# Startup loads, block sizes, buffers, query order and DMA transposes changed together in a windowed-attention plus maxout feed-forward kernel

## The chip, the cores and the metric

The kernel runs on 1 core of one Trainium2 chip. The metric is the device time of one execution in microseconds (us); smaller is better. Engines are named as the profile names them: PE is TensorE's matmuls and PEld its weight loads, DVE is VectorE, ACT is ScalarE, POOL is GpSimd, SP is SyncE (here it only issues DMAs). L317 is line 317 of the kernel that the profile belongs to; the lines of the two kernels differ. The span is the time from the first to the last instruction. A row of slices cuts it into 40 equal parts; each digit is the busy share of a slice in tenths (9 is 90% or more). PEclk is the granted clock, the share of its full speed at which TensorE was allowed to run, in the same tenths; 1.00 is full speed. PSUM is the memory into which TensorE writes its results.

The kernel before takes 196.63 us, the median of the four runs beside the changed kernel (195.34 to 196.85). In longer sessions its executions fall into two groups: of twelve runs of one session six were fast (194.73 to 196.23) and six were called slow, being more than 1.5% above the fastest (197.99 to 200.0). The profiled execution that the prediction reads took 198.22 us and is of the slow group.

## The reference

Attention with a window of 128 keys and 4 sink keys, then a feed-forward layer in which three products compete by maximum:

```python
def _attn_ref(q, k, v, n_sink, window):         # q, k, v: (4, 8, 768, 64) float32
    scores = scale * np.matmul(q, k.transpose(0, 1, 3, 2))
    keep = is_sink | in_window                   # first 4 keys, or 0 <= q - k < 128
    scores = np.where(keep, scores, -1000000000.0)
    a = softmax(scores)                          # written out in the reference
    return np.matmul(a, v)

def _moe_ref(x, w1, w2, w3, w_out):              # x: (3072, 512), w1..w3: (512, 768), w_out: (768, 512)
    h = np.maximum(np.maximum(x @ w1, x @ w2), x @ w3)
    return h @ w_out
```

## The kernel before

The work is cut into 24 tiles of 128 tokens. For two tiles (a chunk of 256 tokens) and one of two head groups of four heads, a unit does: load q and k, transpose them on VectorE, scores on TensorE (`st`), exp on ScalarE, mask on VectorE, PV on TensorE (`o`), normalisation on VectorE (`x`), transpose of x on TensorE (`xt`), copy to `xT` on ScalarE. Some tiles make a block; for a block the feed-forward runs 18 groups of four `h` matmuls and then six `y` matmuls for each tile. Every operation is a task with a wanted time; a small list scheduler in the kernel decides the order in each engine's queue, and each engine works its queue strictly in that order.

```python
    NBUF = 4                                    # chunk buffers of each of q and k
    vbufs = [const.tile([128, H, 6, D + 1], BF16, name=f"v_sb{n}") for n in range(2)]
...
    load("q0.0", 0.26, -2000, qk_first("q", q, 0), eng="SP", cost=2.7)    # first chunk, head group 0
    load("k0.0", 0.26, -2000, qk_first("k", k, 0), eng="ACT", cost=2.7)
    qk_loads(0, 1)                                                        # head group 1, by GpSimd
    t_mask = task("POOL", 2.1, make_masks, want=nxt(), name="mask")
    v_loads(0)
    w_loads(0)
    ...
    for g in range(NQ):
        qk_loads(1, g)
...
    def transposes(ch, g, wants):               # VectorE, on pairs of bf16 taken as one float32
        for nm, want in zip("qk", wants):
            def f(nm=nm):
                src = raw(nm, ch, g).bitcast(F32).rearrange("p (j c) -> p j c", j=8)
                dst = tile_T(nm, ch, g).rearrange("p s e -> p (s e)").bitcast(F32).rearrange(
                    "p (m j) -> p j m", j=8)
                nc.vector.transpose(dst, src)
...
        def xt_copy():
            n = 128 * len(tts)
            src = st["xt"][:, :, 128 * tts[0]:128 * tts[0] + n]
            nc.scalar.copy(xT_tile()[:, 2 * g:2 * g + 2, off:off + n], src)

        def xt_dma(tt):                         # there, but used by no block: FIRST_BY_DMA = 99
            def f():
                o = off + 128 * (tt - tts[0])
                nc.sync.dma_start_transpose(out=xT_tile()[:, :, o:o + 128],
                                            in_=xs_tiles[ch, tt].rearrange("p h d -> p (h d)"))
...
        def store(m):
            def f():
                r = tok0 + 128 * m
                nc.sync.dma_start(out=out[r:r + 128, :], in_=box["ysb", m])
...
BLOCKS = [[0, 1], [2, 3], [4, 5, 6, 7], [8, 9, 10, 11], [12, 13, 14, 15], [16, 17, 18, 19], [20, 21, 22, 23]]
```

GpSimd issues all loads but the first two, with at most eight of them outstanding.

The softmax here doesn't subtract the row's maximum and nothing guards it: scores larger than these inputs give would overflow.

## Time and profile before

| kernel before, profiled execution | |
|---|---|
| span (first to last instruction) | 196.5 us |
| TensorE matmuls busy | 171.2 us, 87% |
| VectorE busy | 129.1 us, 66% |
| ScalarE busy | 95.5 us, 49% |
| GpSimd busy | 55.7 us, 28% |
| first matmul | 9.82 us |
| first y matmul | 38.57 us |

No single share says what bounds the kernel. TensorE is the busiest engine, but its 87% is an average of a first half with holes and a second half that is full. The lines that show it, with their reading, stand in the prediction: the slices, TensorE's waits, the timeline of the hole at 67 to 70 us, and the groups of instructions.

### The profile page before, as it was taken

The numbers are of one execution on the slowest core, as the hardware profiler recorded it, in microseconds if no ns is written. First come the engines' busy times: TensorE is split into PE (matmuls) and PEld (weight loads), VectorE is DVE, ScalarE is ACT, GpSimd is POOL, SyncE is SP. The second block draws the span as 40 slices with busy tenths as digits, with TensorE's granted clock in tenths as the row PEclk, the third lists the DMA queues.
The fourth block names the chain that finished last, engine by engine and source line by source line (L and its number), as shares of the span: only waits on it lengthen the run. The fifth ranks groups of instructions, "written<-read, shape, count | busy, mean of one in ns | idle before, by whom it ended". The sixth has DMA issues, their size and how long they took to land.

```text
span 196.5 us, 4237 instructions
## 1 busy us (share of the span) xinstructions
PE 171.2 (87%) x1659; PEld 95.6 (49%) x1680; DVE 129.1 (66%) x289; ACT 95.5 (49%) x147; POOL 55.7 (28%) x83
## 2 busy tenths in 40 slices
PE   0067978399999779999999999999999999999992
PEld 0044766148764335554445644555544556444440
DVE  4457768539999188998499962896915588135520
ACT  3263555436673606775175374736861573432222
POOL 7996759343692260059120000000000000000000
PEclk9999999969999969999999999999999999999999
DMA  5999999999999969099992023000041000230014
GB/s 113 127 162 164 196 182 173 172 136 215 127 135 136 139 69 175 24 71 142 243 153 43 3 81 132 3 0 3 0 168 49 2 3 0 107 112 0 0 53 160
DMA packets 58964, 19.52 MB, mean 99 GB/s; under 512 B 44352, under 2 KB 55616, under 8 KB 58944
## 3 DMA queue, kind: packets, MB, share of 16 engines
q0 software_dynamic: 54592, 12.40, 71.6%
q1 hardware_dynamic: 4160, 6.59, 9.4%
q10 hardware_dynamic: 192, 0.26, 0.4%
q8 instruction: 13, 0.21, 0.4%
q14 instruction: 7, 0.06, 0.1%
HBM read 25.17 MB, written 6.29 MB: 160 GB/s over the span
## 4 chain that ended last, share of the span: by engine, by line
PE 47%; DMA 27%; issue 11%; POOL 9%; SPq 3%; DVE 1%; ACT 0%; POOLq 0%; ACTq 0%
PE h L562 29%; DMA q_raw<-in_q_dram 16%; PE y L581 11%; DMA v_sb<-in_v_dram 6%; DMA w_sb<-in_moe_w_dram 5%; SPq L335 3%; PE o L442 3%; PE st L412 2%; POOL w_sb L199 2%; POOL v_sb L290 2%; PE xt L471 2%; POOL q_raw L188 1%; POOL k_raw L188 1%; PE o L433 1%; POOL v_sb L194 1%
## 5 line engine op out<-in xcount | busy, mean ns | idle before, releaser
L562 PE MATMUL h<-xT,w_sb 128*128 128x512 bf16 (+1 forms) x489 | 106.4, 355 | 3.0 <-DMA w_sb<-in_moe_w_dram 1.1
L573 DVE TENSOR_TENSOR h_sb<-h,h_sb 128x512 bf16<-128x512 f32 (+1 forms) x84 | 51.3, 610 | 35.5 <-PE h L562 32.1
L562 PEld LDWEIGHTS <-w_sb 128*128 128x128 bf16 x504 | 46.5, 100 | 39.2 <-issue 2.9
L417 ACT ACTIVATE e_sb<-st 128x1024 bf16<-128x1024 f32 (+1 forms) x48 | 44.0, 953 | 16.7 <-PE st L412 15.8
L571 ACT CAST h_sb<-h 128x512 bf16<-128x512 f32 (+1 forms) x42 | 22.1, 526 | 41.5 <-PE h L562 41.5
L581 PE MATMUL y<-wo_sb,h_sb 128*128 128x512 bf16 x138 | 34.3, 394 | 3.5 <-DMA wo_sb<-in_moe_w_out_dram 3.1
L424 DVE TENSOR_TENSOR e_sb<-e_sb,mask 128x1024 bf16<-128x1024 bf16 (+1 forms) x48 | 29.7, 638 | 2.4 <-ACT e_sb L417 2.4
L412 PE MATMUL st<-qT,kT 32*128 32x128 bf16 (+1 forms) x512 | 15.4, 248 | 9.9 <-DVE kT L302 9.8
L581 PEld LDWEIGHTS <-h_sb 128*128 128x128 bf16 x144 | 14.1, 101 | 19.6 <-issue 5.3
L588 ACT COPY y_sb<-y 128x512 f32<-128x512 f32 x24 | 14.1, 587 | 19.5 <-PE y L581 17.1
L302 DVE STREAM_TRANSPOSE qT<-q_raw 128x256 f32<-128x256 f32 x24 | 15.0, 633 | 11.8 <-DMA q_raw<-in_q_dram 11.8
L461 DVE TENSOR_TENSOR x<-o,rc 128x256 bf16<-128x256 f32 x48 | 20.4, 425 | 1.7
L442 PEld LDWEIGHTS <-e_sb 128*128 128x128 bf16 x352 | 16.9, 99 | 8.9 <-DVE e_sb L424 2.5
L483 ACT COPY xT<-xt 128x512 bf16<-128x512 bf16 x24 | 14.1, 588 | 13.9 <-PE xt L471 13.7
L442 PE MATMUL o<-v_sb,e_sb 128*128 128x65 bf16 x352 | 18.9, 197 | 1.6 <-DVE e_sb L424 1.4
L188 POOL DMA_DIRECT2D k_raw<-in_k_dram x23 | 15.6, 678 | 14.0 <-DVE x L461 4.5
L188 POOL DMA_DIRECT2D q_raw<-in_q_dram x23 | 15.9, 691 | 12.9 <-DVE h_sb L573 4.3
L412 PEld LDWEIGHTS <-kT 32*128 32x128 bf16 x512 | 10.2, 96 | 15.0 <-DVE kT L302 9.8
L302 DVE STREAM_TRANSPOSE kT<-k_raw 128x256 f32<-128x256 f32 x24 | 14.7, 627 | 1.1 <-DMA k_raw<-in_k_dram 1.1
L471 PE MATMUL xt<-ident,x 128*128 128x128 bf16 x96 | 12.3, 229 | 1.7 <-DVE x L461 1.7
L290 POOL DMA_DIRECT2D v_sb<-in_v_dram x6 | 8.7, 1445 | 13.9 <-PE st L412 11.9
L471 PEld LDWEIGHTS <-x 128*128 128x128 bf16 x96 | 7.7, 100 | 9.4 <-DVE x L461 3.6
(34 smaller groups left out, 48.3 us busy)
## 6 DMA issues: line engine op xcount, KB each, us to landing
out_dram<-y_sb SPq DMA_DIRECT2D x24, 256.0 KB
q_raw<-in_q_dram POOLq DMA_DIRECT2D x23, 128.0 KB, 9.6
k_raw<-in_k_dram POOLq DMA_DIRECT2D x23, 128.0 KB, 8.8
w_sb<-in_moe_w_dram POOLq DMA_DIRECT2D x9, 256.0 KB, 8.1
v_sb<-in_v_dram POOLq DMA_DIRECT2D x6, 384.0 KB, 11.5
vbd<-v_sb SPq DMA_DIRECT2D x64, 0.5 KB
v_sb<-in_v_dram POOLq DMA_DIRECT2D x6, 128.0 KB, 7.6
wo_sb<-in_moe_w_out_dram POOLq DMA_DIRECT2D x1, 768.0 KB, 10.0
```

Source lines behind the costliest of these rows:

```text
L188: nc.gpsimd.dma_start(out=raw(nm, ch, g), in_=s)
L302: nc.vector.transpose(dst, src)
L412: nc.tensor.matmul(ps[:, i, col:col + n], lhsT=kk[r, k0:k0 + 128, e], rhs=qT[r, q0:q0 + n, e], start=(e == 0), stop=(e == 1))
L417: nc.scalar.activation(st["e"][:, :, cols(tt)], st["ps"][:, :, cols(tt)], AF.Exp, scale=scale)
L424: nc.vector.tensor_tensor(out=ee, in0=ee, in1=m.unsqueeze(1).to_broadcast(list(ee.shape)), op=ALU.mult)
L442: nc.tensor.matmul(o[:, i, :], lhsT=st["e"][:, i, col:col + 128], rhs=vbufs[b % 2][:, 4 * g + i, kb, :], start=(c == 0 and n == 0), stop=( ...
L461: nc.vector.tensor_tensor(out=x, in0=o[:, :, :D], in1=rc.unsqueeze(2).to_broadcast([128, 4, D]), op=ALU.mult)
L471: nc.tensor.transpose(st["xt"][:, n, 128 * tt:128 * tt + 128], x[:, 128 * n:128 * n + 128], ident)
L562: nc.tensor.matmul(ps[:, :ntok], lhsT=w_sb[:, wi, d, fb * 128:fb * 128 + 128], rhs=xTs[blk][:, d, :ntok], start=(d == 0), stop=(d == DSUB ...
L571: nc.scalar.copy(hs, ps[:, :ntok])
L573: nc.vector.tensor_tensor(out=hs, in0=ps[:, :ntok], in1=hs, op=ALU.max)
L581: nc.tensor.matmul(ps, lhsT=box["h"][:, fb, 128 * m:128 * m + 128], rhs=wo_sb[:, fb, :], start=(fb == 0), stop=(fb == FSUB - 1))
```

## The change

The intent is to start sooner, to keep TensorE supplied until all loads are in, and to take work off TensorE where it is the bound. Six things change at once:

- q and k of the first chunk come for both head groups in four pieces each over three queues (SP, ACT, GpSimd), and the masks are built mostly by VectorE;
- the loads are reordered: chunk 1 before the first input weights;
- eight chunk buffers instead of four, and v of all four batches in tiles of its own;
- blocks of 2, 2, 2, 4, 4, 4, 4, 2 tiles instead of 2, 2, 4, 4, 4, 4, 4;
- x of the last three blocks (10 tiles) is transposed by DMA;
- the queries are in a permuted order within a tile, so that VectorE's transpose writes runs of 16 words; ScalarE's copy of x undoes the order, and in the DMA-transposed blocks the store of y undoes it.

```diff
+    load("q0.0", 0.26, -2000, qk_first("q", q, 0, nc.sync), eng="SP", cost=1.8)
+    load("k0.0", 0.26, -2000, qk_first("k", k, 0, nc.scalar), eng="ACT", cost=1.8)
+    load("q0.1", 0.26, -1999, qk_first("q", q, 1, nc.sync), eng="SP", cost=1.8)
...
-    NBUF = 4
+    NBUF = 8
-    vbufs = [... for n in range(2)]
+    vbufs = [... for n in range(B)]
...
-    qk_loads(0, 1)
-    t_mask = task("POOL", 2.1, make_masks, want=nxt(), name="mask")
+    load("k0.1", 0.26, nxt(), qk_first("k", k, 1, nc.gpsimd), cost=2.4)
     v_loads(0)
-    w_loads(0)
     for g in range(NQ):
         qk_loads(1, g)
     v_loads(1)
+    w_loads(0)
...
+                if nm == "q":
+                    dst = dst.rearrange("p (s j m) -> p j s m", s=2, j=8)
+                    src = src.rearrange("p (j s m) -> p j s m", j=8, s=2)
...
-            nc.scalar.copy(xT_tile()[:, 2 * g:2 * g + 2, off:off + n], src)
+            src = st["xt"][...].rearrange("p n (s j m) -> p n s m j", j=8, m=16)
+            dst = xT_tile()[...].rearrange("p n (s m j) -> p n s m j", j=8, m=16)
+            for t in range(len(tts)):
+                nc.scalar.copy(dst[:, :, t], src[:, :, t])
...
-                nc.sync.dma_start(out=out[r:r + 128, :], in_=box["ysb", m])
+                to = out[r:r + 128, :]
+                if blk >= FIRST_BY_DMA:
+                    to = to.rearrange("(m j) d -> j m d", j=8)
+                nc.sync.dma_start(out=to, in_=box["ysb", m])
...
-BLOCKS = [[0, 1], [2, 3], [4, 5, 6, 7], [8, 9, 10, 11], ..., [20, 21, 22, 23]]
-LEAD = 6.0
-FIRST_BY_DMA = 99
+BLOCKS = [[0, 1], [2, 3], [4, 5], [6, 7, 8, 9], [10, 11, 12, 13], [14, 15, 16, 17], [18, 19, 20, 21], [22, 23]]
+LEAD = 5.0
+FIRST_BY_DMA = 5
```

Cut from it: the mask code, the cost figures of the scheduler's model (which also move the order a little), and options that are switched off in both kernels (`N_BY_PE`, `TWO`).

## The prediction

> **What bounds the kernel now.** I read the page's slices first, then TensorE's waits, then 5 us stretches around each wait, then the timeline inside the worst one, then the groups of instructions. The slices (40 of 4.9 us, busy in tenths):
>
> ```profile
> PE   0067978399999779999999999999999999999992
> ...
> PEclk9999999969999969999999999999999999999999
> DMA  5999999999999969099992023000041000230014
> ```
>
> Two kernels stand one after the other here. From slice 21 (about 100 us) TensorE is full at full clock and the DMA engines are nearly idle. Before that TensorE has holes, the DMA row is at 9, and the two places where the granted clock falls come just behind holes. For the second part the busy table says the same in one line (columns: span, then busy us of PE, PEld, DVE, ACT, POOL, then clock):
>
> ```profile
> 100.00:193.00 93.00, 92.23 (x785) 47.61 (x796) 57.84 (x119) 45.32 (x71) 0.67 (x1) 1.00 0.17 48
> ```
>
> Only less TensorE work can shorten those 93 us. Most of what is lost lies before. TensorE's own waits up to 100 us:
>
> ```profile
> PE st L412 <- DVE kT L302: 9.8, 1, 9.8
> PE y L581 <- DMA wo_sb<-in_moe_w_out_dram: 3.1, 1, 3.1
> PE o L433 <- DVE h_sb L573: 1.9, 1, 1.9
> ```
>
> The first is the start: TensorE can begin at 9.82 us, when the last of four query/key transposes is done. The second is the arrival of the output weights at 38.57 us: block 0 is finished and its output product stands in front of everything else. The third is named "DVE h_sb", but the timeline shows what held VectorE:
>
> ```profile
> 66.38 1.02 PE L562 MATMUL h<-xT,w_sb 128*128 128x512 bf16 x4
> ...
> 68.10 0.64 DVE L302 STREAM_TRANSPOSE qT<-q_raw 128x256 f32<-128x256 f32 x1 [4.16 <-DMA q_raw<-in_q_dram]
> 68.59 0.67 DVE L573 TENSOR_TENSOR h_sb<-h,h_sb 128x512 bf16<-128x512 f32 x1
> ...
> 69.31 0.27 PE L433 MATMUL o<-vbd,e_sink 128*128 128x260 bf16 x1 [1.90 <-DVE h_sb L573]
> ```
>
> VectorE stood 4.16 us at the head of its queue on a transpose whose query chunk had not landed, the maxima behind it could not empty PSUM, and TensorE stopped. The chunk was issued at 58.66 and took 9.4 us to land, which is the median for queries (9.6); what was late is the issue: with four buffers per stream GpSimd waited there, the timeline says, for a transpose of VectorE. Both holes have an echo:
>
> ```profile
> 35.00:40.00 5.00, 1.80 (x28) 0.91 (x18) 1.98 (x6) 1.94 (x2) 1.43 (x3) 0.91 2.16 167
> 40.00:45.00 5.00, 5.00 (x45) 2.74 (x44) 2.62 (x7) 2.54 (x6) 2.00 (x3) 0.75 3.42 137
> ...
> 65.00:70.00 5.00, 2.88 (x37) 1.59 (x31) 1.90 (x5) 2.52 (x3) 1.58 (x3) 0.98 1.06 117
> 70.00:75.00 5.00, 4.58 (x32) 2.01 (x35) 4.37 (x11) 0.79 (x2) 1.74 (x3) 0.68 0.72 78
> ```
>
> The stretch after each hole runs at clock 0.75 and 0.68.
>
> **What the Trainium skill says.** (1) "TensorE: Matmul & The Clock Gate", What's actually happening: the default state is throttled, activity releases it, and an idle window brings it back. The trace agrees in kind: full clock elsewhere, 0.75 and 0.68 after the holes at 35 to 38.6 and 67 to 70 us. (2) "DMA: Bandwidth & Descriptors", Issuing engines are not separate DMA queues: starting DMAs from several engines only saves issue time. The trace before cannot show it for the first loads, but its DMA row is at 9 from slice 2 to slice 15, so three queues should bring the first tiles sooner and the last of the startup bytes no sooner. (3) "VectorE: DVE Perf Modes", The three transpose paths: a 128x128 bf16 transpose takes 390 ns on TensorE, 1309 ns on the DMA crossbar. The trace has 229 ns per transpose matmul and no DMA transpose; a longer latency off the engines is what the change buys.
>
> **The unit costs.** From spacings in the timeline at full clock: h matmul of 512 columns 0.216 us (72 from 172.03 to 187.57), of 256 columns 0.110 (8 from 50.76 to 51.64), y 0.216; scores of one unit (4 heads, one chunk) 0.57, or 0.46 in the first chunk of a batch; PV of a 128-token tile 0.37, in first chunks about 0.19; one transpose pair 0.11; sink scores 0.35. Total: h 432 x 0.216 = 93.3; y 144 x 0.216 = 31.1; scores 16 x 0.57 + 8 x 0.46 = 12.8; PV 32 x 0.37 + 16 x 0.19 = 14.9; transposes 48 x 0.11 = 5.3; sinks 5 x 0.35 = 1.8. Sum 159.2 us. Of it 14.8 lie before 38.57 us (72 h of 256 columns 7.9, six score units 3.2, eight PV tiles 2.2, seven pairs 0.8, two sinks 0.7). The other 144.4 take from 38.57 to 193.0, 154.4 us: 10.0 lost. Of these 2.5 are the hole at 67 to 70, and the clock costs (1 - 0.92) x 21.4 = 1.7 from 38.6 to 60 and (1 - 0.91) x 20 = 1.8 from 60 to 80; 4.0 are small waits.
>
> **The change part by part.**
> - Start. First chunks of both head groups come over SP, ACT and GpSimd, and VectorE transposes head group 0 first (in the kernel before, group 1's pair went first and TensorE used group 0). The casts end at 7.43 and 7.94; two transposes at 0.5 us spacing let TensorE start at about 8.6, some 1.2 us sooner. The masks, 6 GpSimd instructions of 0.3 us, become 2 there and 4 on VectorE, which idles 3.9 us then: free.
> - Order of loads. The bytes up to the output weights are the same 11 MB (six q/k groups, v of batch 0, all weights), and the DMA engines are full, so the weights should still land near 38.5. But block 2 is now 256 tokens and TensorE's order puts 108 h matmuls, not 72, before the first y: 36 x 0.11 = 4.0 us, plus one transpose pair 0.1. TensorE was ready at 35.4 and will start 1.2 sooner, so it is ready at about 38.3: the 3.1 us wait is filled, and 18.9 us of work are done at 38.6.
> - Buffers. With eight chunk buffers and all four v tiles no load waits for a transpose or a PV. The hole at 67 to 70 (2.5 us) goes, and with both holes most of their clock loss: I keep 1.0 of 3.5 us.
> - DMA transposes. Blocks 5 to 7 are 10 of 24 tiles: 20 pairs x 0.11 = 2.2 us less on TensorE, in the stretch where it is the bound, so it counts in full. ACT loses 10 copies of 0.588 us; the other 14 become 28 smaller ones (about 0.37 each, the duration of a 128x256 cast), 10.4 for 8.2 us: no matter at 49% busy.
> - Permuted queries. They let x come out in an order that ACT's copy or the store undoes; VectorE's query transpose then writes runs of 16 words. No row shows what that saves; I take nothing.
> - Blocks of 256: two more, 144 matmuls x (0.110 - 0.108) = 0.3 us more.
>
> Sum: remaining after 38.6 = 159.2 - 2.2 + 0.3 - 18.9 = 138.4. Lost: small waits 4.0, clock 1.0. TensorE ends at 38.6 + 143.4 = 182.0. The tail after it (last y copy and store, 3.5 us) stays: span 185.5. The timed median stands 0.3 over the span before: 185.8.
>
> **The rivals.**
> (a) VectorE takes over between 30 and 66 us. These are the rows:
>
> ```profile
> L573 DVE TENSOR_TENSOR h_sb<-h,h_sb 128x256 bf16<-128x256 f32 x24 | 10.0, 417 | 3.9 <-PE h L562 3.0 <-DVE h_sb L573 0.5
> L424 DVE TENSOR_TENSOR e_sb<-e_sb,mask 128x1024 bf16<-128x1024 bf16 x40 | 26.7, 682 | 0.7 <-ACT e_sb L417 0.7
> L302 DVE STREAM_TRANSPOSE qT<-q_raw 128x256 f32<-128x256 f32 x24 | 15.0, 633 | 11.8 <-DMA q_raw<-in_q_dram 11.8
> ```
>
> By the changed order VectorE has, from block 0's last maximum to block 2's, 24 maxima (10.0 us), 16 transposes (spaced 0.49 back to back: 7.8), 11 + 2 masks (8.3), 13 normalisations of 0.60 (7.8), 2 small ones: 34 us. TensorE has 31 for the same. For it: VectorE would end near 64, just where TensorE's own sum ends, so any wait for a chunk costs. Against it: it had 9 us of idle there before. I add 0.7 to the centre; fully, it makes 189.
> (b) The DMA transposes are late. Between the last PV of each of blocks 5, 6 and 7 and its first h stand 24 y matmuls, 5.2 us, in which normalisation (1 us), issue and transfer of the last tile must pass. If one takes over 4 us, each of three blocks loses 1 to 3 us, plus clock: 189 to 193. The skill's 1309 ns per 128x128, four to a tile but over 16 engines, speaks for it being tight but enough.
> (c) The wait only moves: the startup is bound by bytes, w_in for block 0 now comes after chunk 1, and v's 256-byte pieces are slow. If the output weights slip by 3 us, 189. If the DMA runs better than before (fewer issue waits), 183.
>
> **Range and chances.** Centre 186.5. Rivals (a) to (c) each add about 3 and rarely all together; below, nothing beats 138.4 + 3.5 after a landing near 38, about 180. Range 182 to 191.5. Faster by over 2% means under 192.9: 0.91; within 2% 0.08; slower 0.01, which would need transposes that stall every block.
>
> **What would show it.** Right: first matmul near 8.6; the first y right at the landing of the output weights, without 3 us idle; no wait of VectorE for q_raw over 2 us after 40; clock at 0.9 or more in every slice after the start; 56 transpose matmuls instead of 96; the stretch after 100 us full. Wrong: waits of h on the DMA transposes (b), VectorE above 95% between 40 and 66 with TensorE waiting for h_sb (a), or a first y much after 39 (c).

## The result, and the profile after

The changed kernel takes 190.13 us (median of four runs, 189.62 to 191.62, all fast). The ratio to the kernel before is 0.9695, with a 95% interval from 0.9623 to 0.9767. Here and below a ratio is the mean time of one kernel's fast runs over that of the other's of the same rounds, so it is not quite the ratio of the medians. The profiled execution took 190.57 us and has a span of 188.9 us.

The slices of the changed kernel, 40 of 4.7 us, answer to the three rows that the prediction shows of before:

```profile
PE   0267898899899999999999999999999999999970
...
PEclk9999999999999999999999999999999999999996
DMA  5989999999999999999997011250040440014403
```

The two dips of the granted clock are gone; only the last slice, in which TensorE has finished, is lower. The holes of TensorE are gone too: from the fifth slice on no digit is under 8 until the end. The DMA row is full until about 100 us, as before. The last digits differ: TensorE's row ends with "70", where before ended with "92", so the changed kernel has a longer stretch at the end in which TensorE does nothing.

Busy time in three stretches (columns: span, then busy us and instructions of PE, PEld, DVE, ACT and POOL, then clock, DMA share, GB/s):

```profile
30.00:40.00 10.00, 8.64 (x130) 6.59 (x128) 7.34 (x20) 5.30 (x12) 5.25 (x7) 1.00 1.55 176
40.00:69.20 29.20, 27.88 (x395) 20.98 (x398) 25.22 (x69) 18.68 (x37) 18.21 (x24) 1.00 2.09 153
69.20:183.00 113.80, 112.84 (x976) 60.50 (x989) 77.53 (x171) 53.22 (x87) 17.48 (x23) 1.00 0.58 84
```

The clock is full in all three. From 69.2 us, the first y matmul of block 2, TensorE is busy 112.84 of 113.8 us. Between 40 and 69.2 us VectorE is busy 25.22 of 29.20 us (86%), below the 95% that the prediction named as the sign of rival (a).

The waits (engine, line, what it waited for; us in all, times, longest):

```profile
PE st L435 <- DVE kT L317: 7.3, 1, 7.3
DVE qT L317 <- DMA q_raw<-in_q_dram: 3.4, 4, 1.2
...
PE h L588 <- DVE h_sb L602: 1.0, 2, 0.7
```

The start is at 7.3 instead of 9.8 us. VectorE's waits for query chunks fall from 11.8 us with a longest of 4.2 to 3.4 us with a longest of 1.2. The 3.1 us wait of y for the output weights is no longer among the waits of over half a microsecond. No wait of h for a DMA transpose is in the list.

The permuted order shows in the duration of VectorE's query transposes (before: 633 ns, shown in the prediction), and the two small copies of x in ScalarE's group:

```profile
L317 DVE STREAM_TRANSPOSE qT<-q_raw 128x256 f32<-128x256 f32 x24 | 10.3, 432 | 4.5 <-DMA q_raw<-in_q_dram 3.4
...
L510 ACT COPY xT<-xt 128x256 bf16<-128x256 bf16 x28 | 9.1, 380 | 7.0 <-PE xt L495 7.0
L495 PE MATMUL xt<-ident,x 128*128 128x128 bf16 x56 | 7.7, 231 | 1.6 <-DVE x L485 1.5
```

The end needs a closer look. The timeline of the changed kernel's last 9 us (start, duration, engine, line, operation), then that of the kernel before:

```profile
180.18 2.75 PE L616 MATMUL y<-wo_sb,h_sb 128*128 128x512 bf16 x11
...
182.33 1.89 SPq L633 DMA_DIRECT2D out_dram<-y_sb  x2
183.02 0.59 ACT L623 COPY y_sb<-y 128x512 f32<-128x512 f32 x1 [0.71 <-PE y L616]
```

```profile
189.72 4.22 SPq L595 DMA_DIRECT2D out_dram<-y_sb  x4
...
193.00 0.59 ACT L588 COPY y_sb<-y 128x512 f32<-128x512 f32 x1 [0.71 <-PE y L581]
```

After: the last copy ends at 183.61 and the span at 188.9, 5.3 us later. Before: the last copy ends at 193.59 and the span at 196.5, 2.9 us later. The DMA engines' busy share over the last stretch shows most of it; first the changed kernel from 170 to 189 us, then the kernel before from 180 to 197 us, each in 40 slices:

```profile
DMA  0670443555455454542000000000253455452000
```

```profile
DMA  0000000000000000000000001940950950950000
```

Each store of before is a short burst in which nearly all engines work: 9 tenths, up to 386 GB/s. The permuted stores of after never pass 5 tenths and 207 GB/s in these slices, so they last twice as long and run into each other. (The digits 6 and 7 at the start of the first row belong to a DMA transpose.) The Trainium skill, "DMA: Bandwidth & Descriptors", section "Why a DMA increments its semaphore by 16 and not by 1", says that a transfer is spread over the largest number of engines, at most 16, that divides the slowest dimension of both its sides. The permuted output `j m d` has 8 as its slowest dimension, so 8 of 16 engines. The trace agrees: half the busy share, half the rate. A small part, 0.26 us, is the issue: the last two stores of the changed kernel occupy SyncE from 182.33 us for 1.89 us, those of e3 below, with plain stores and the same two copies in front, for 1.63 us.

### The profile page after: what moved, and what is told of

Read it like the earlier page. It is cut to its first block, busy times and chain, and to the rows that moved or that the text cites. A ratio compares the mean times of both kernels' runs of the same rounds, so it can differ in the third digit from the quotient of the medians.

```text
span 188.9 us, 4359 instructions
## 1 busy us (share of the span) xinstructions
PE 167.7 (89%) x1693; PEld 100.4 (53%) x1712; DVE 128.3 (68%) x307; ACT 91.3 (48%) x158; POOL 63.2 (33%) x93
## 4 chain that ended last, share of the span: by engine, by line
PE 62%; DMA 21%; POOL 7%; DVE 4%; issue 2%; ACT 0%; DVEq 0%; ACTq 0%; POOLq 0%
PE h L588 38%; DMA q_raw<-in_q_dram 15%; PE y L616 14%; DMA w_sb<-in_moe_w_dram 6%; PE st L435 4%; PE o L466 4%; POOL w_sb L204 2%; POOL v_sb L199 2%; DVE h_sb L602 2%; PE o L457 1%; POOL k_raw L183 1%; PE xt L495 1%; DVE kT L317 1%; DVE x L485 1%; DVE e_sb L448 1%
## 5 line engine op out<-in xcount | busy, mean ns | idle before, releaser
L588 PE MATMUL h<-xT,w_sb 128*128 128x256 bf16 (+1 forms) x565 | 105.1, 331 | 2.6 <-DVE h_sb L602 1.0
L602 DVE TENSOR_TENSOR h_sb<-h,h_sb 128x256 bf16<-128x256 f32 (+1 forms) x96 | 52.7, 554 | 32.9 <-PE h L588 20.6
L588 PEld LDWEIGHTS <-w_sb 128*128 128x128 bf16 x576 | 54.2, 100 | 37.0 <-issue 2.8
L597 ACT CAST h_sb<-h 128x256 bf16<-128x256 f32 (+1 forms) x48 | 23.2, 484 | 45.3 <-PE h L588 45.2
L199 POOL DMA_DIRECT2D v_sb<-in_v_dram x24 | 21.9, 913 | 7.3 <-DMA q_raw<-in_q_dram 3.7
L317 DVE STREAM_TRANSPOSE qT<-q_raw 128x256 f32<-128x256 f32 x24 | 10.3, 432 | 4.5 <-DMA q_raw<-in_q_dram 3.4
L485 DVE TENSOR_TENSOR x<-o,rc 128x256 bf16<-128x256 f32 x28 | 11.9, 424 | 1.0
L510 ACT COPY xT<-xt 128x256 bf16<-128x256 bf16 x28 | 9.1, 380 | 7.0 <-PE xt L495 7.0
L476 DVE RECIPROCAL rc<-o 128x4 f32<-128x4 f32 x48 | 8.3, 174 | 3.5 <-PE o L466 3.5
L495 PE MATMUL xt<-ident,x 128*128 128x128 bf16 x56 | 7.7, 231 | 1.6 <-DVE x L485 1.5
```

Of the source, the lines that this page charges most:

```text
L199: nc.gpsimd.dma_start(out=vbufs[b][:, :, n, :D], in_=s[:, n])
L588: nc.tensor.matmul(ps[:, :ntok], lhsT=w_sb[:, wi, d, fb * 128:fb * 128 + 128], rhs=xTs[blk][:, d, :ntok], start=(d == 0), stop=(d == DSUB ...
L597: nc.scalar.copy(hs, ps[:, :ntok])
L602: nc.vector.tensor_tensor(out=hs, in0=ps[:, :ntok], in1=hs, op=ALU.max)
```

## The experiments

Twelve kernels ran, all with right results. "Control" is the unchanged changed kernel, run again in the first session: 190.82 us. The other sessions have no control, but the kernel before ran in each, and the mean of its fast runs was 195.3 to 195.6 us in all four (196.4 beside the first result), so times of different sessions are compared directly. Most edits are relative to the changed kernel. The first table gives times, the second milestones of the profiled executions.

| run | edit | median (range) us | ratio [95%] |
|---|---|---|---|
| e1 | none (control) | 190.82 (190.13 to 191.67) | 0.9773 [0.9738, 0.9809] |
| e3 | natural query order, DMA transposes kept | 188.26 (187.74 to 189.56) | 0.9652 [0.9611, 0.9694] |
| e2 | last block: order undone in h's operand | 215.52 (214.62 to 217.22) | 1.1042 [1.099, 1.1094] |
| e4 | no DMA transposes | 192.09 (191.58 to 192.91) | 0.9841 [0.981, 0.9873] |
| e7 | head group 1's first chunk by plain GpSimd loads | 194.52 (193.99 to 196.3) | 0.9972 [0.987, 1.0075] |
| e8 | load order of before | 191.68 (190.67 to 192.22) | 0.9792 [0.9717, 0.9866] |
| e10 | block sizes of before | 200.84 (200.49 to 201.78) | 1.0285 [1.0213, 1.0357] |
| e5 | four chunk buffers | 190.66 (190.31 to 191.22) | 0.9748 [0.9678, 0.9818] |
| e6 | four chunk buffers and two v tiles | 191.01 (189.35 to 191.64) | 0.975 [0.9665, 0.9836] |
| e11 | kernel before with the new buffers only | 197.93 (197.46 to 198.27) | 1.0127 [1.0059, 1.0196] |
| e9 | twelve maxima moved partly to ScalarE | 191.71 (191.04 to 195.82) | 0.9786 [0.9685, 0.9887] |
| e12 | e3 plus block 4 by DMA, and a split last tile | 197.93 (196.26 to 198.88) | 1.0121 [1.0053, 1.0189] |

| us | first y | first y of block 2 | last y group starts | last two apart |
|---|---|---|---|---|
| changed kernel | 40.05 | 69.20 | 180.18 | 110.98 |
| e1 | 39.24 | 69.91 | 180.89 | 110.98 |
| e3 | 40.45 | 69.27 | 180.25 | 110.98 |
| e5 | 39.92 | 69.70 | 180.68 | 110.98 |
| e6 | 40.92 | 69.91 | 180.90 | 110.99 |
| e7 | 40.57 | 72.83 | 183.35 | 110.52 |
| e8 | 37.06 | 69.23 | 181.25 | 112.02 |
| e9 | 40.15 | 69.97 | 181.60 | 111.63 |
| e4 | 39.48 | 69.54 | 183.85 | 114.31 |

The second table is worth keeping in mind for what follows. With the new block sizes and the DMA transposes, the stretch from block 2's first y to the last y group is 110.5 to 112.0 us in all rows whose x still goes by DMA. So an edit that acts early counts mainly if it moves that point, which stands near 69 to 70 us in all rows but one; in e8 and e9 about 1 us was lost after it.

### e1: the control

> Control: the changed kernel once more, as the yardstick of this job. Both theories: 190.1 us, within 1. In its profile 5.4 us from the end of the last y copy to the end of the span, against 2.9 in the kernel before.

The span is 189.6 us; the last copy ends at 184.31, 5.3 us before the end, as in the first profile. The long tail is no accident of one execution. The gain over the kernel before is 2.3% beside this control, with six fast runs of each, and 3% beside the first result, with four of each; the two intervals just overlap, so the gain is better put at 2 to 3%.

### e3: natural query order

```diff
-                base=0, pattern=[[1, 8], [8, 16]], channel_multiplier=-1)     # mask in permuted order
+                base=0, pattern=[[16, 8], [1, 16]], channel_multiplier=-1)    # in natural order
-                if nm == "q":        # the permuting pattern of the query transpose
+                if False:
-            for t in range(len(tts)):
-                nc.scalar.copy(dst[:, :, t], src[:, :, t])
+            nc.scalar.copy(xT_tile()[:, 2 * g:2 * g + 2, off:off + n], st["xt"][...])
-                if blk >= FIRST_BY_DMA:
-                    to = to.rearrange("(m j) d -> j m d", j=8)
```

> Queries in natural order, transposes by DMA kept: no permutation anywhere, so all stores are plain. Theory half-engines: tail shorter by 2 to 2.5 us; VectorE's 24 query transposes go back from 0.43 to 0.63 us, 4.8 us more busy, of which up to 1.5 shows in the dense stretch from 40 to 66 us; 188 to 189.3. Rival (the permutation was needed, VectorE bounds the middle): 191 or more.

The time is 188.26 us, 2.6 under the control, and the DMA row over 170 to 187 us has its bursts back:

```profile
DMA  0771999973920000000000000000000870770000
```

The last copy ends at 183.68 and the span at 186.8: a tail of 3.1 us instead of 5.3. VectorE's query transposes are back at 0.631 us each, 15.0 us in all instead of 10.3, and block 2's first y still stands at 69.27. So the permutation bought 4.7 us of VectorE's time, none of which reached the end, and cost 2.2 us at the store. This kernel beats both the kernel before and the changed kernel.

### e2: the order undone in the operand of h

The first idea was to give the last block a plain store by undoing the order in an operand of TensorE. In the stationary operand it did not build (that operand takes one free dimension), so the moving operand of the last block's h matmuls reads x with a step of 16 elements:

```diff
+            r = xTs[blk][:, d, :ntok]
+            if blk == len(BLOCKS) - 1:
+                r = r.rearrange("p (t j m) -> p t m j", j=8, m=16)
-                if blk >= FIRST_BY_DMA:
+                if FIRST_BY_DMA <= blk < len(BLOCKS) - 1:
```

> The last block's tokens are put back in order by the moving side of its h matmuls, so its two stores have 128 rows as their outermost size again. Theory half-engines (the permuted store has outermost size 8, runs on half of the DMA engines, and two such stores pile up in the tail): the tail shrinks by 2 to 2.5 us, 187.8 us, 0.987 of the control. Rival (the tail grew because it now follows the shorter block or lands more slowly for another reason): 190, no change of the tail. If the strided moving operand is slow, the last block's 72 h matmuls (7.9 us) grow instead.

The time is 215.52 us, a miss by far. The group of the last block's h matmuls in the timeline, and the clock's row:

```profile
171.01 33.28 PE L594 MATMUL h<-xT,w_sb 128*128 128x256 bf16 x72
```

```profile
PEclk9999999999999999999999999999999995555558
```

72 matmuls took 33.28 us, 0.46 us each, where the same matmuls with a contiguous operand take 0.11. TensorE's row stays at 9 over this stretch, so by its own account it is working; the granted clock reads 5 tenths. The factor of four is the step, not the clock, as the trace settles. These are the h matmuls of the last block in two stretches (columns: span, then busy us and instructions of PE, DVE and ACT, then clock, DMA share, GB/s):

```profile
171.00:174.00 3.00, 2.99 (x7) 0.00 (x0) 0.37 (x1) 1.00 0.48 143
177.00:204.00 27.00, 27.00 (x60) 3.98 (x10) 1.86 (x5) 0.50 0.01 3
```

At full clock 7 matmuls fill 3 us, at half clock 60 fill 27 us: about 0.45 us each in both. The clock falls only at 175 us, some 4 us after the slow matmuls began, and it does not change their pace. The Trainium skill, "SBUF — State Buffer", section "Door 1: The DMA port swizzle", says that a read that crosses to a new 16-byte line pays a penalty; with a step of 32 bytes each element does. The trace agrees in direction, and the page has no size for it. The tail, with a plain store for the last block only, is 3.1 us from the end of the last copy (210.09) to the end of the span (213.2) instead of 5.3. That agrees with the half-engines theory, though the last two copies lie 2.56 us apart here instead of 1.30, so e3 is the cleaner test.

### e4: no DMA transposes

```diff
-FIRST_BY_DMA = 5
+FIRST_BY_DMA = 99
```

> No DMA transposes (all x through TensorE, ACT puts the order back, stores plain). Theory: TensorE gets 20 pairs of 0.11 us back, +2.2, the tail loses 2 to 2.5, so 190.0 within 0.7: the DMA transposes as built are worth nothing net. Rival (the DMA path also removes waits on ACT and PSUM): 192 or more.

192.09 us, 1.3 over the control; 190.0 was expected. The last y group starts 3.0 us later than in the control. The 20 pairs of transposes that TensorE gets back are worth 2.2 us by the prediction's 0.11 each. The waits of h for ScalarE's copy of x rise from 0.5 to 1.3 us, which would be the other 0.8. The tail shrinks to 3.2 us, because without DMA transposes the store is plain. So the DMA transposes gave 3.0 us on TensorE and the store that came with them took 2.2 back.

### e7: the first chunk of head group 1 by plain GpSimd loads

```diff
-for nm, g in (("q", 0), ("k", 0), ("q", 1)):
+for nm, g in (("q", 0), ("k", 0)):
-    load("q0.1", 0.26, -1999, qk_first("q", q, 1, nc.sync), eng="SP", cost=1.8)
-    load("k0.1", 0.26, nxt(), qk_first("k", k, 1, nc.gpsimd), cost=2.4)
-    ...
+    qk_loads(0, 1)
```

> Only head group 0's first chunk over SP and ACT; group 1's by two ordinary GpSimd loads, as before. Theory: the startup is bound by the landing of the output weights near 40 us, so a start later by 1 to 2 us is absorbed: 190.3 to 191, first y still near 40. Rival: the start counts in full, 191.8 or more.

194.52 us, 3.7 over the control. The timeline of the first 11 us:

```profile
7.68 0.62 ACT L318 CAST q_raw<-q_f 128x512 bf16<-128x512 f32 x1 [3.50 <-DMA q_f<-in_q_dram]
...
10.62 0.61 PE L432 MATMUL st<-qT,kT 32*128 32x256 bf16 x8 [10.62 <-DVE kT L314]
```

The cast of the first queries starts at 7.68 instead of 5.42 us, although the loads that it waits for are issued as before; only the loads beside them changed. The first matmul comes at 10.62 instead of 7.29. Of these 3.3 us the cast explains 2.3; for the rest VectorE has head group 1's transposes in the same queue and stands 0.69 us at one whose k has not landed. I had thought that a late start would be absorbed by the wait for the output weights. It is not: the first y stands at 40.57 (changed kernel: 40.05), but it has only 80 h matmuls in front of it instead of 108, the clock is 0.85 between 30 and 40 us (1.00 in the changed kernel), and block 2's first y is at 72.83, 2.9 us later than in the control. That the first loads are late because whole-chunk loads run beside them is argued from the timing, not tested further.

### e8: the load order of before

```diff
     v_loads(0)
+    w_loads(0)
+    t_bd = task("POOL", 0.6, make_bd, want=nxt(), name="bd")
     for g in range(NQ):
         qk_loads(1, g)
     v_loads(1)
-    w_loads(0)
-    t_bd = task("POOL", 0.6, make_bd, want=nxt(), name="bd")
```

> The load order of the kernel before (first third of the weights ahead of chunk 1). Theory: same bytes up to the output weights, which land at 40 either way; h starts some 2 us earlier, the first y does not: within 0.7 of 190.5. Rival c of the prediction: the new order costs or gains at the first y more than 1 us.

191.68 us, 0.9 over the control. The first h starts at 14.58 us, 4.5 earlier than in the control, and the first y at 37.06, 2.2 us earlier. Little of this lasts: between 40 and 60 us TensorE is busy 17.60 of 20 us at clock 0.91 (control: 17.53 at clock 1.00), and block 2's first y stands at 69.23 (control: 69.91). Work done sooner on the feed-forward of block 0 seems to be only moved: what block 2 waits for has not come any sooner. That is argued, not tested.

### e10: the block sizes of before

```diff
-BLOCKS = [[0, 1], [2, 3], [4, 5], [6, 7, 8, 9], [10, 11, 12, 13], [14, 15, 16, 17], [18, 19, 20, 21], [22, 23]]
+BLOCKS = [[0, 1], [2, 3], [4, 5, 6, 7], [8, 9, 10, 11], [12, 13, 14, 15], [16, 17, 18, 19], [20, 21, 22, 23]]
```

> The changed kernel with the block sizes of before (2, 2, 4, 4, 4, 4, 4 tiles instead of 2, 2, 2, 4, 4, 4, 4, 2; DMA transposes then cover 8 tiles, not 10). Theory of the prediction: fewer h matmuls stand before the first y, TensorE waits there some 3 us for the output weights and the clock dips: 193.5 to 195. Rival: block sizes do not matter once the start is earlier: 190.5 to 191.5 (0.4 of it the two tiles).

200.84 us: 10.0 over the control, and 2.9% slower than the kernel before; both expectations (at most 195) were far off. The holes are back, and the timeline shows them as it did for before:

```profile
63.32 0.45 DVE L317 STREAM_TRANSPOSE qT<-q_raw 128x256 f32<-128x256 f32 x1 [2.97 <-DMA q_raw<-in_q_dram]
...
69.95 0.45 DVE L317 STREAM_TRANSPOSE qT<-q_raw 128x256 f32<-128x256 f32 x1 [3.02 <-DMA q_raw<-in_q_dram]
...
71.03 0.27 PE L457 MATMUL o<-vbd,e_sink 128*128 128x260 bf16 x1 [3.54 <-DVE h_sb L602]
```

VectorE stands 3 us at a query transpose whose chunk has not landed, twice; the maxima behind it cannot run, and TensorE stops for 3.54 us. Four 128-token tiles in block 2 mean that two chunks must be in before block 2's h can start. This kernel has eight chunk buffers and four v tiles, so it is not a shortage of buffers. With two tiles in block 2, TensorE has 72 h matmuls (7.9 us) and 12 y matmuls more to do while the next chunks come; this reading is argued from the timeline. Between 60 and 80 us TensorE is busy 14.05 us at clock 0.91, against 19.62 at clock 1.00 in the control. Not all of the 10.0 us is holes: the last block has four permuted stores here, and the tail after the last copy is 6.2 us instead of 5.3.

### e5 and e6: fewer buffers in the changed kernel

```diff
-    NBUF = 8
+    NBUF = 4                                             # e5 and e6
-    vbufs = [... for n in range(B)]
+    vbufs = [... for n in range(2)]                      # e6; loads of batch b wait for the PVs of b - 2
```

> The changed kernel with four chunk buffers instead of eight, all of v still on chip. Theory buffers: loads wait for VectorE's transposes again, a chunk lands late and VectorE stands on it as before at 64 to 68 us: a TensorE hole of 2 us or more between 40 and 100 us with a fall of the clock behind it, 193 or more against 190.5. Rival: the chunks' times are set by the load order and the DMA rate, not by free buffers: 190 to 191, no such hole.

> Four chunk buffers and two v buffers, as in the kernel before (v of batch 2 and 3 waits for the PV of batch 0 and 1). Theory buffers: 193.5 to 195, the hole at its full size of 2.5 us plus 1.5 of clock. Rival: as e5, 190 to 191. If e5 shows nothing and this does, v was the part that counted.

190.66 and 191.01 us: no effect of either. GpSimd does wait for VectorE in e5, up to 3.1 us at a time, and TensorE does not notice it.

### e11: the new buffers in the kernel before

```diff
-    NBUF = 4
+    NBUF = 8
-    vbufs = [... for n in range(2)]
+    vbufs = [... for n in range(B)]
```

(on the kernel before; the loads of a batch then wait for no PV)

> The kernel before with eight chunk buffers and all four v tiles on chip, nothing else. Theory of the prediction: the hole at 67 to 70 us and its clock fall go, 2.5 to 4 us faster: ratio 0.980 to 0.987. Rival (as e5 and e6 say of the changed kernel): within 0.5% of before, and the hole moves or stays.

197.93 us, ratio 1.0127. All four runs count as fast by their own fastest, but they lie where the slow group of the kernel before begins, so I read this as "no gain", not as a loss. The hole has not moved:

```profile
68.57 0.64 DVE L303 STREAM_TRANSPOSE qT<-q_raw 128x256 f32<-128x256 f32 x1 [3.95 <-DMA q_raw<-in_q_dram]
...
69.78 0.27 PE L434 MATMUL o<-vbd,e_sink 128*128 128x260 bf16 x1 [1.69 <-DVE h_sb L574]
```

Against before: 3.95 us instead of 4.16, and 1.69 instead of 1.90. The chunk in question was issued at 59.03 us (58.66 before). With buffers free, the issue is no earlier.

### e9: VectorE relieved

The kernel has a switch by which the second of an h group's two maxima is taken from a copy that ScalarE makes:

```diff
-TWO = {}
+TWO = {1: (0, 1, 2, 3, 4, 5), 2: (0, 1, 2, 3, 4, 5)}
```

> In blocks 1 and 2 ACT copies the second h group of each of the six feature blocks out of PSUM and VectorE takes the maximum of two SBUF tiles: 12 of VectorE's maxima of 0.42 us become about 0.21, ACT gets 12 copies of 0.38 (it is 63% busy there). Theory VectorE (rival a: VectorE sets the pace from 47 to 69 us, where it is busy without a gap for 13 us): the first y of block 2 comes 1.5 to 2.5 us sooner (67 to 68 instead of 69.2 to 69.9), the end moves with it, 188.6 against 190.5. Rival (arrival of the chunks sets it, VectorE only queues behind them): less than 0.6 us.

191.71 us (one of four runs was slow), no gain. The twelve maxima took 0.28 us each instead of 0.42, so the relief was 1.7 us and not the 2.5 expected. VectorE's waits for query chunks rise from 3.4 to 6.6 us in all, with a longest of 3.0, and block 2's first y stands at 69.97. What VectorE saves it spends waiting for chunks.

### e12: an attempt at a better kernel

On e3, block 4 is also transposed by DMA, and the last y tile is copied in halves by ScalarE and VectorE and stored in halves over two queues:

```diff
-FIRST_BY_DMA = 5
+FIRST_BY_DMA = 4
+                if blk == len(BLOCKS) - 1 and m == ntok // 128 - 1:
+                    nc.scalar.copy(y_sb[:, :256], box["y", m][:, :256])
+                    nc.vector.tensor_copy(y_sb[:, 256:], box["y", m][:, 256:])
```

> The run in natural order with the DMA transposes (188.26 us median, ratio 0.9652) gets two additions: block 4's x is also transposed by DMA (14 of 24 tiles instead of 10; 36 or 40 transpose matmuls instead of 56), and the last y tile is copied in two halves by ScalarE and VectorE and stored in two halves over two queues. Theory (TensorE is the bound after 70 us, and the tail counts in full): 8 pairs x 0.11 = 0.9 us less on TensorE, and 0.4 to 0.6 less tail (the last copy takes 0.59, half of it 0.35; the half store is no shorter in latency), so 186.5 to 187.1, ratio about 0.956. Rival (block 4's DMA transposes come while loads of batch 3 still fill the DMA engines, and stand behind 16 small transfers of the sink values on SyncE's queue): h of block 4 waits for the last of them by 1 us or more, the milestone of block 4's first y does not move, and the time is 188 to 189.5.

197.93 us, slower than the control by 7 and than e3 by 9.7. The rival was right about the queue and far too mild. SyncE's queue up to 103 us, then TensorE:

```profile
88.29 10.69 SPq L350 DMA_DIRECT2D vbd<-v_sb  x16
99.10 3.90 SPq L513 DMA_TRANSPOSE xT<-xd  x3
```

```profile
105.76 0.58 PE L586 MATMUL h<-xT,w_sb 128*128 128x512 bf16 x1 [8.45 <-DMA xT<-xd]
```

The transposes stand in SyncE's queue behind 16 small transfers of sink values, which take it until 98.98 us. The last x of block 4 was ready at 92.44 us; its four transposes are issued from 99.10 to 104.36. TensorE waits 8.45 us for them, and the clock is 0.83 on average from 100 to 130 us, the end of the wait included. Whether the loads that still ran beside the transposes slowed them too, as the rival also said, was not separated. The split tail gave nothing either: the two half copies ran one after the other (ScalarE's from 193.38 to 193.75, VectorE's from 193.78 to 194.21), together longer than the one copy of 0.59 us, and the span ended 3.9 us after TensorE. So the best kernel is e3.

## Why the prediction was right or wrong

Right: 190.13 us lies in 182.0 to 191.5, and the kernel is faster by 3% (2.3% beside the control). The centre, 186.5, was 3.6 us too low. The sum by its own terms, against the profiled execution of 190.57 us:

| term | predicted | measured |
|---|---|---|
| first matmul | 8.6 | 7.29 |
| first y | 38.6 | 40.05 |
| from there to TensorE's end | 143.4, or 144.1 with the 0.7 for rival (a) | 142.9 |
| TensorE's end | 182.0, or 182.7 | 182.9 |
| "the tail after it (last y copy and store, 3.5 us) stays" | 3.5 | 6.0 |
| "the timed median stands 0.3 over the span" | 0.3 | 1.7 |

**Start.** Right in direction. The first matmul came 1.3 us sooner still, because the casts started at 5.42 instead of 6.81 us; I had kept their times of before. e7 shows that this part is worth 3.7 us of the total, more than the 1.2 us by which I counted it: what it feeds is the point at 69 us, not only the first y.

**First y and the weights.** The 3.1 us wait was filled, as said. The weights landed 1.4 us later than assumed: their load, issued at 28.99, took 11.0 us instead of 10.0. This is half of rival (c). In e8 the weights landed by 37.06 and nothing was gained, though chunk 1 was loaded later there.

**Clock.** Right: no dip after the start.

**TensorE's sum.** Right to 1 us. The full stretch behind the first y came out as counted, with 56 transposes instead of 96, and e4 puts the DMA transposes at 3.0 us on TensorE, of which I had counted 2.2. Rival (b), late transposes, did not happen for blocks 5 to 7. e12 shows that it was no idle fear: one block earlier TensorE waits 8.45 us. That TensorE's end came out within 0.2 us is in part luck: the first y was 1.4 us late, and the stretch behind it 1.2 us short of the 144.1.

**Tail: the first failed term.** I wrote that it stays at 3.5 us, and did not ask what the permuted store does. It is a part of the change with a direct cost: half the DMA engines, a tail of 6.0 us. e3, which takes the permutation out, brings back a tail of 3.1 us after the last copy and gains 2.6 us.

**From span to timed run: the second failed term.** The 0.3 came from comparing a median with the span of an execution of the slow group. Compared execution by execution, the timed figure is 1.7 us above the span: 190.57 over 188.9, 191.62 over 189.9, 189.62 over 187.9, and for the profile of before 198.22 over 196.5. The two failed terms, 2.5 and 1.4 us, with 0.2 on TensorE's end, make up the 4.1 us between 186.5 and 190.57.

**Buffers: a wrong cause, and a right size by luck.** The prediction put the hole at 67 to 70 us down to "four buffers per stream", and took the hole away for that reason. The hole did go, but e11 gives the kernel before all the buffers and keeps the hole, and e5 and e6 take the buffers from the changed kernel and get no hole. e10 shows which part of the change removed the hole: the block sizes. With them undone, the holes return in spite of all the buffers, and 10.0 us are lost. In the prediction the smaller block 2 served only to fill the wait at the first y, some 3 us.

**Permuted queries.** "I take nothing" was right for VectorE's share: 4.7 us less busy, no gain. Rival (a), VectorE as the bound, is not shown: relieving it by 1.7 us (e9) gained nothing. One reading of the prediction is slightly off, without consequence: in the DMA row of before, slice 15 stands at 6 and not at 9.

The parts do not add up to the whole. Undoing one at a time costs 10.0 (blocks), 3.7 (first loads), 0.9 (order), 1.3 (DMA transposes with their store), 0 (buffers) and gains 2.6 (permutation), a sum of 13.3, where the whole change gives 6. With the block sizes of before, all the rest together, the new cost figures of the scheduler included, is a loss.

**What stays open.** No fast execution of the kernel before was profiled. The one with the hole at 67 to 70 us took 198.22 us, 2.6 to 2.9 us above the mean of the fast ones in the four sessions, and all runs of e11, which has the hole too, lie there as well. So it is not known whether the hole belongs to the kernel or only to its slower group. What holds block 2's first y at 69 to 70 us is not settled. It is not buffers (e5, e6), hardly the landing of the output weights (e8, where the load order changed with it), and not VectorE's work alone (e9). The DMA row stands at 9 up to there, at most eight loads are outstanding, and VectorE must take chunks in queue order; that the rate of arrival paces it fits all runs, but no run changed that rate by itself. Nor did a run separate the scheduler's changed cost figures from the rest.

## What to carry to other kernels

Follow a layout trick to its far end before counting it: here a faster transpose on an engine with time to spare was paid for by a store whose outermost dimension of 8 halved its DMA engines, at the one place where nothing lies beside it. Where loads still come in, ask what TensorE can do between two arrivals; the size of a block set that here, and more buffers did not. And before giving an in-order queue one more latency-bound job, look at what stands in front of it there.

## What the Trainium skill lacked or had wrong

- "DMA: Bandwidth & Descriptors", section "Issuing engines are not separate DMA queues": it says that transfers of several engines interleave, and gives no size for what this costs the transfer that is waited for. In e7 the first loads are issued from 0.81 us as in the changed kernel, so their issue time is the same, but with whole-chunk loads by GpSimd beside them instead of pieces over three queues the first cast came 2.3 us later and the kernel was 3.7 us slower.
- The same page, "Why a DMA increments its semaphore by 16 and not by 1": its rule on the number of engines held here, and it gives no rate for a store on half of them. In these runs it was 5 tenths of busy share and at most 207 GB/s for 8 rows outermost, 9 tenths and up to 386 GB/s for 128.
- "SBUF — State Buffer", section "Door 1: The DMA port swizzle": it gives the penalty for leaving a 16-byte line no size for TensorE or VectorE. In these runs a 128x256 matmul with a moving operand in 32-byte steps took 0.46 us instead of 0.11 (at clock 1.00 as at 0.50), and VectorE's 128x256 transpose 0.63 us when it writes words in 32-byte steps, 0.43 when it writes runs of 16 words.
- "VectorE: DVE Perf Modes", section "The three transpose paths": it gives 1309 ns for a 128x128 transpose by DMA, and nothing on the time that the issuing queue is taken. Here the issue of a 128x512 one took SyncE 1.2 us (median), and three hidden blocks turned into a stall of 8.45 us when the queue held 16 small transfers in front.
- No page gives the step from the span between the first and the last instruction to the timed figure of an execution: 1.65 to 1.83 us in every execution here.
